# One V of each layer loads its last 512 columns in sixteen transfers of eight rows

## The chip, the cores and the metric

The kernel runs on one core of one Trainium2 chip. The metric is the time of one execution on the device in microseconds; of several executions the median is given. A profile of one execution gives what each engine did and when.

The engines named below are PE (TensorE, matmuls), DVE (VectorE), ACT (ScalarE), POOL (GpSimd) and SP (SyncE, which here only issues DMA transfers). Behind SP stand 16 transfer engines that move the bytes.

## The reference

One token goes through two layers, each an attention over a cache of 4096 positions in 32 heads and an MLP with a hidden width of 1376. All data are float32. Both layers read the same caches and weights.

```python
def _A_ref(x, k_cache, v_cache, wq, wo):
    q = (x @ wq).reshape(B, Sq, H, Dh).transpose(0, 2, 1, 3)
    scores = jnp.einsum("bhqd,bhkd->bhqk", q, k_cache) * (Dh ** -0.5)
    p = _softmax(scores, axis=-1)
    o = jnp.einsum("bhqk,bhkd->bhqd", p, v_cache)
    return o.transpose(0, 2, 1, 3).reshape(B, Sq, H * Dh) @ wo

def _B_ref(x, w1, b1, w2, b2):
    h = _gelu(jnp.einsum("bsd,df->bsf", x, w1) + b1)
    return jnp.einsum("bsf,fd->bsd", h, w2) + b2

x = x + _A_ref(_layernorm(x), ...)
x = x + _B_ref(_layernorm(x), ...)
...
```

(The last two lines are run twice.)

## The kernel before

The 32 heads are cut into G = 8 groups of four heads. A group's K is one block of 128 rows x 16384 columns (64 KiB a row, 8 MiB), laid out with the head's width on the rows; its V is a block of the same size with the cache's positions on the rows. Beside them come 2 MiB per group of query and output weights, called w. A block has C = 8 chunks of NC = 2048 columns, a chunk has four pieces of U = 512 columns, one per head or position block.

All of it lies in one SBUF tensor, `arena`, whose places are given by column: three homes of one block each, and behind them room for w and for scratch. `load` (L83) issues one transfer on SP into given columns of all 128 rows. Layer 0 goes through the groups upwards, layer 1 downwards, so that the last groups of layer 0 are reused; n counts the groups within a layer.

For each n the program does, in this order: load K of this group (issued ahead), `scores` (L213: 64 matmuls on PE, chunk by chunk), `softmax` (L217 to L233), load V and `values` (L241: again chunk by chunk), load w, `scaled_out` (L245 to L250), `head_out` (L269, reads wo), and `queries` for the next group (L203 to L208, reads wq). In layer 0 the homes of K and V go round among the three; in layer 1 V has home 0 and K home 1. `stream` (L356) issues a block's load and hands out its chunks; for a V in the middle of a layer it is a single transfer of the whole block (`WHOLE`).

SP takes its transfers in the order of the program, and each can carry waits: for readers of the place that it overwrites, and for a semaphore. The transfers of SP count on eight semaphores in turn, DMAHW0 to DMAHW7: transfer number i (from 0) counts on DMAHW(i mod 8), and before a semaphore is used again, the transfer that used it last must have landed. In the kernel before there are 79 transfers.

Of the kernel before, what the change touches and what calls it, by code (L numbers as in the profile page):

```python
# [23 lines left out]
C = 8  # L24
# [3 lines left out]
U = 512  # L28
KEPT = 6

NC = 4 * U
BLOCK = 8 * NC
# [21 lines left out]
WHOLE, HALVES = ((0, 8),), ((0, 4), (4, 8))  # L54
# [4 lines left out]
def decode_layers(ctx: ExitStack, tc: tile.TileContext, k, v, w, w1, w2, out):  # L59
    nc = tc.nc  # L60
# [20 lines left out]
    arena = const.tile([P, ARENA], F32, name="arena")  # L81

    def load(at, src):  # L83
        t = arena[:, at : at + src.shape[-1]]
        tc.keep_in_program_order(nc.sync.dma_start(t, src))
        return t
# [4 lines left out]
    def chunk(t, i=0):  # L91
        return t[:, NC * i : NC * (i + 1)].rearrange("p (j n) -> p j n", j=4)

    def of_w(first, n):

        row, i = first
        return w[row][:, AHEAD + NC * i : AHEAD + NC * (i + n)]

    def wq_at(g):
        return (g + 1) % 2, g  # L100

    def wo_at(g):
        return g % 2, g

    def free_now(layer, n):

        if layer == 0:
            at = HELD + 2 * NC
        elif n == 0:
            at = 6 * NC  # L110
            return arena[:, at : at + U], arena[:, 11 * NC : 11 * NC + 4 * 129]
        else:
            at = 9 * NC if n == 1 else 2 * BLOCK + NC
        return arena[:, at : at + U], arena[:, at + U : at + U + 4 * 129]
# [6 lines left out]
    def part(src, g, a, b):  # L121

        return src[g][:, NC * a : NC * b]
# [115 lines left out]
    def values(i, pt, vt, c, of=C):  # L239
        for j in range(J):  # L240
            nc.tensor.matmul(pO[32 * j : 32 * j + 4, :], pt[:, j, c, :], by_head(vt)[:, j],  # L241
                             start=(i == 0), stop=(i == of - 1))

    def scaled_out(rl, ot):
        nc.vector.transpose(ot[:, :512], pO)  # L245
        diag = ot.rearrange("p (b q) -> p b q", q=129)[:, :, :P]
        diag = diag.rearrange("p b (d q) -> p d b q", q=32)[:, :, :, 0]
        o, on = small("o", 4), small("on", 4)
        nc.vector.tensor_reduce(o, diag, axis=AX.X, op=ALU.add)
        nc.vector.tensor_scalar(on, o, rl, None, op0=ALU.mult)  # L250
        return on
# [101 lines left out]
    nc.gpsimd.tensor_copy(b2c, ahead[:, B2_AT : B2_AT + 4])  # L353
    here = {}

    def stream(what, g, pieces, base):  # L356

        for a, b in pieces:
            t = load(base + NC * a, part(k if what == "k" else v, g, a, b))
            for c in range(a, b):  # L360
                here[what, g, c] = chunk(t, c - a)
                yield c, here[what, g, c]

    w1_t = arena[:, HELD:PAIR]
    w2_t = [[arena[:, at : at + U] for at in homes] for homes in W2_AT]

    def idle(t, at, n=512):
        pin(nc.tensor.matmul(at[:C, :n], ident[:, :C], t[:, 0, :n], start=True, stop=True))  # L368

    for layer in range(2):  # L370
# [22 lines left out]
        for n, g in enumerate(order):  # L393
            first, final = n == 0, n == G - 1

            k_home, v_home = ((2 * n + i) % 3 * BLOCK for i in (1, 2))
            if layer == 1:
                k_home, v_home = K2_HOME if n == 2 else BLOCK, 0

            if layer == 1 and n == 0:  # L400
                tiles = [(c, here["k", g, c]) for c in range(C)]
            elif layer == 1 and n == 1:
                tiles = [(c, here["k", g, c]) for c in range(2)]
                tiles += list(stream("k", g, ((2, 4), (4, 8)), -2 * NC))
                n_kept = STAY + U * KEPT
                load(V1_HOME[6] + n_kept % NC, v[g][:, n_kept:BLOCK])
                for u in range(STAY, n_kept - U, U):
                    nc.scalar.copy(v_next(u), pK[(u - STAY) // U])
                for c in range(STAY // NC, C):
                    here["v", g, c] = chunk(arena[:, V1_HOME[c] : V1_HOME[c] + NC])  # L410
            elif layer == 1 and n == 2:
                tiles = [(c, here["k", g, c]) for c in range(6)]
                tiles += list(stream("k", g, ((6, 8),), 2 * BLOCK - 6 * NC))
            else:
                tiles = stream("k", g, HALVES if first or final else WHOLE, k_home)
# [5 lines left out]
            p, ot = free_now(layer, n)  # L421
# [7 lines left out]
            if layer == 1 and n == 0:  # L429
                for c in range(C):  # L430
                    values(c, pt, here["v", g, c], c)
            elif layer == 1 and n == 1:
                for c in range(C):
                    values(c, pt, here["v", g, c], c)

                for pieces, base in ((((0, 4),), K2_HOME), (((4, 6),), SPARE - 4 * NC)):
                    for _ in stream("k", order[2], pieces, base):
                        pass
            elif final:
                last_v = chunk(arena[:, v_home + BLOCK - NC : v_home + BLOCK])  # L440
                for _ in range(FILL - 1):
                    idle(t, pS)
                for c, t in stream("v", g, LAST, v_home):
                    values(c, pt, t, c, C - 1)
                    if c == C - 2:
                        others = scaled_out(rl, ot)
                    for _ in range(LAST_IDLE.get(c, 0)):
                        idle(t, pS)
                for a in (BLOCK - NC, BLOCK - NC // 2):
                    load(v_home + a, v[g][:, a : a + NC // 2])  # L450
                for c in range(C):
                    here["v", g, c] = chunk(arena[:, v_home + NC * c : v_home + NC * (c + 1)])
            else:
                for c, t in stream("v", g, WHOLE, v_home):
                    for i in range(KEPT - 1):
                        if layer == 0 and n == G - 2 and c == (STAY + U * i) // NC:
                            nc.scalar.copy(pK[i], t[:, STAY // U % J + i - J * (c - STAY // NC), :])
                    values(c, pt, t, c)
# [3 lines left out]
            elif final:  # L462
                at = PAIR + NC * layer
# [8 lines left out]
            else:  # L472
                t = load(PAIR, of_w(wo_at(g) if layer == 0 else wq_at(g - 1), 2))
# [23 lines left out]
        at = work.tile([P, P], F32, name="pt")  # L497
# [18 lines left out]
        if layer == 0:  # L516
# [4 lines left out]
            g = G - 2  # L521
# [53 lines left out]
```

## Time and profile before

| | |
|---|---|
| Time, median of 3 runs | 678.17 us (677.4 to 679.03) |
| Profiled execution, its own time | 677.63 us |
| Its span, first to last instruction | 675.9 us |
| Busy: PE, DVE, ACT, POOL | 408.1, 115.2, 27.4, 5.0 us |
| Read from HBM | 284.92 MB, 422 GB/s over the span |
| Chain that ended last, by engine | PE 40%, DMA 39%, unknown queue 14% |
| Granted TensorE clock, mean | 0.806 |

The views used are: the page's slices (the span in 40 equal parts, each digit the busy tenths), its rows on DMA queues and on DMA issues (KB each, median us from issue to landing), the windows (busy time of each engine in a stretch, then granted clock, DMA share and GB/s), the chain of waits in order of time (start, length, what), the timeline of SP (start, length of the issue, what it loads) and the list of who waited for whom. "Landing" is the moment at which the last of a transfer's engines has reported.

### The profile page before, as it was taken

What the parts mean: (1) busy time and instruction counts of PE and PEld (TensorE: products, weight loads), DVE (VectorE), ACT (ScalarE), POOL (GpSimd) and SP (SyncE); (2) the same over time, 40 slices, a digit from 0 to 9 for tenths busy, and PEclk for the clock granted to TensorE, in tenths of its full rate; (3) what the DMA queues carried; (4) which work ended last, traced back from release to release, by engine and by line L of the source; (5) the groups of instructions that cost most, each with busy time, mean ns of one, the idle gap of its engine ahead of it and who ended that gap; (6) DMA issues with size and microseconds to landing.
All of it is one profiled execution on the core that took longest, in us unless ns stands there. A gap on an engine that the chain in (4) does not pass through costs nothing.

```text
span 675.9 us, 6740 instructions
## 1 busy us (share of the span) xinstructions
PE 408.1 (60%) x3008; PEld 109.8 (16%) x3008; DVE 115.2 (17%) x369; ACT 27.4 (4%) x57; POOL 5.0 (1%) x24
## 2 busy tenths in 40 slices
PE   2745664565534854467597986674466545755596
PEld 1111111111111111111124321111111111111123
DVE  3002110120021201212022322120121111200212
ACT  0010000000000000001011200000000000000010
POOL 1000000000000000000000000000000000000000
PEclk9779776797678865878899998976797767976899
DMA  9999999999999999999999999999999999999995
GB/s 374 435 434 434 435 435 434 413 457 432 428 427 422 444 434 432 434 432 417 433 410 353 427 418 462 407 447 435 426 432 431 432 434 409 461 432 411 426 414 234
DMA packets 11268, 285.34 MB, mean 422 GB/s; under 512 B 1252, under 2 KB 1256, under 8 KB 3688
## 3 DMA queue, kind: packets, MB, share of 16 engines
q1 hardware_dynamic: 11240, 284.92, 98.6%
q8 instruction: 23, 0.38, 0.2%
q14 instruction: 5, 0.04, 0.0%
HBM read 284.92 MB, written 0.00 MB: 422 GB/s over the span
## 4 chain that ended last, share of the span: by engine, by line
PE 40%; DMA 39%; another core or an unknown queue 14%; DVE 4%; ACT 1%; issue 1%; ACTq 0%; SPq 0%; DVEq 0%
DMA arena<-in_v 35%; PE pO L241 19%; PE pS L213 12%; DMA arena<-in_w 4%; PE pB L269 4%; PE pO L207 1%; PE pO L225 1%; ACT arena L223 1%; PE pS L368 1%; DVE arena L245 1%; DVE smalls L217 1%; PE pO L368 0%; PE pO L343 0%; DVE arena L205 0%
## 5 line engine op out<-in xcount | busy, mean ns | idle before, releaser
L213 PE MATMUL pS<-arena,smalls 128*8 128x512 f32 x1024 | 148.3, 732 | 112.5 <-DMA arena<-in_k 111.6
L241 PE MATMUL pO<-arena,pt 128*4 128x512 f32 x1008 | 139.9, 700 | 79.1 <-DMA arena<-in_v 78.6
L269 PE MATMUL pB<-arena,smalls 128*1 128x512 f32 x112 | 52.8, 616 | 21.9 <-DVE smalls L250 15.9
L213 PEld LDWEIGHTS pS<-arena,smalls 128*8 128x8 f32 x1024 | 30.1, 103 | 214.9 <-issue 190.9
L241 PEld LDWEIGHTS pO<-arena,pt 128*4 128x4 f32 x1008 | 28.4, 95 | 178.0 <-issue 175.2
L217 DVE TENSOR_REDUCE smalls<-pS 128x1 f32<-128x512 f32 x16 | 11.1, 692 | 253.1 <-PE pS L213 253.1
L245 DVE STREAM_TRANSPOSE arena<-pO 128x512 f32<-128x512 f32 x16 | 11.5, 717 | 217.1 <-PE pO L241 217.1
L223 ACT ACTIVATE arena<-pS,smalls 128x512 f32<-128x512 f32 x16 | 12.4, 778 | 536.2 <-DVE smalls L222 536.2
L205 DVE SCALAR_TENSOR_TENSOR arena<-arena,smalls 128x512 f32<-128x512 f32 x45 | 33.8, 752 | 1.6
L225 PE MATMUL pO<-ident,arena 128*128 128x128 f32 x64 | 13.2, 341 | 33.8 <-ACT arena L223 33.5
L269 PEld LDWEIGHTS pB<-arena,smalls 128*1 128x1 f32 x112 | 8.6, 85 | 65.9 <-issue 38.2
L207 PE MATMUL pO<-smalls,arena 128*128 128x1 f32 x120 | 16.6, 259 | 3.3 <-DVE arena L205 3.3
L207 PEld LDWEIGHTS pO<-smalls,arena 128*128 128x128 f32 x120 | 15.3, 200 | 15.5 <-DVE arena L205 13.8
L225 PEld LDWEIGHTS pO<-ident,arena 128*128 128x128 f32 x64 | 8.5, 169 | 47.7 <-ACT arena L223 46.5
L368 PE MATMUL pO<-arena,ident 128*8 128x512 f32 (+1 forms) x38 | 15.9, 547 | 0.0
L368 PE MATMUL pS<-arena,ident 128*8 128x512 f32 (+1 forms) x34 | 14.0, 517 | 0.5 <-DVE pt L307 0.5
L203 DVE TENSOR_SCALAR arena<-arena,smalls 128x512 f32<-128x512 f32 x15 | 7.2, 480 | 4.7 <-DMA arena<-in_w 4.7
L343 PE MATMUL pO<-arena,smalls 128*1 128x128 f32 x176 | 5.9, 272 | 3.3 <-DMA arena<-in_w 2.2
L208 DVE COPY smalls<-pO 128x4 f32<-128x4 f32 x15 | 2.5, 165 | 26.5 <-PE pO L207 26.5
L169 PE MATMUL pO<-smalls 128*32 128x1 f32 x64 | 2.0, 184 | 7.4 <-DVE smalls L163 6.3
L229 DVE STREAM_TRANSPOSE smalls<-smalls 128x32 f32<-128x32 f32 x16 | 3.4, 211 | 17.5 <-ACT arena L223 17.5
L295 PE MATMUL pS<-arena,smalls 128*2 128x128 f32 (+1 forms) x160 | 4.9, 259 | 1.9 <-DMA arena<-in_w 1.9
(92 smaller groups left out, 101.2 us busy)
## 6 DMA issues: line engine op xcount, KB each, us to landing
arena<-in_k SPq DMA_DIRECT2D x8, 4096.0 KB, 26.0
arena<-in_w SPq DMA_DIRECT2D x13, 2048.0 KB, 33.2
arena<-in_v SPq DMA_DIRECT2D x2, 4096.0 KB, 38.4
arena<-in_k SPq DMA_DIRECT2D x3, 2048.0 KB, 15.9
arena<-in_v SPq DMA_DIRECT2D x2, 2048.0 KB, 41.6
arena<-in_w SPq DMA_DIRECT2D x4, 1024.0 KB, 16.3
arena<-in_w SPq DMA_DIRECT2D x6, 512.0 KB, 13.3
arena<-in_v SPq DMA_DIRECT2D x2, 1024.0 KB, 43.2
```

The source lines that it names most:

```text
L203: pin(nc.vector.tensor_scalar(t, wt[:, 0, :], xc[:, 0:1], None, op0=ALU.mult))
L205: nc.vector.scalar_tensor_tensor(t, wt[:, c, :], xc[:, c : c + 1], t, op0=ALU.mult, op1=ALU.add)
L207: nc.tensor.matmul(at[:, j : j + 1], t[:, P * j : P * (j + 1)], one, start=True, stop=True)
L213: nc.tensor.matmul(pS[32 * j : 32 * j + C, :], z[:, j, C - 1 - c : 2 * C - 1 - c], kt[:, j, :], start=(c == 0), stop=(c == C - 1))
L217: nc.vector.tensor_reduce(mx[:, 0:1], pS, axis=AX.X, op=ALU.max)
L223: nc.scalar.activation(p, pS, AF.Exp, bias=bias[:, 0:1], scale=sc, accum_out=mx[:, 0:1])
L225: nc.tensor.transpose(pT[:, b].rearrange("p j r -> p (j r)"), p[:, P * b : P * (b + 1)], ident)
L241: nc.tensor.matmul(pO[32 * j : 32 * j + 4, :], pt[:, j, c, :], by_head(vt)[:, j], start=(i == 0), stop=(i == of - 1))
L245: nc.vector.transpose(ot[:, :512], pO)
L269: nc.tensor.matmul(pB[0:1, :], on[:, d : d + 1], wt[:, d, :], start=n == 0 and d == 0, stop=n == G - 2 and d == 3)
L343: pin(nc.tensor.matmul(pM[32 * j : 32 * j + 1, :], g[:, c - b0 : c - b0 + 1], w2_t[c][:, P * j : P * (j + 1)], start=(c == 0), stop=(c == ...
L368: pin(nc.tensor.matmul(at[:C, :n], ident[:, :C], t[:, 0, :n], start=True, stop=True))
```

## The change

Two V blocks, that of n = 3 in layer 0 and that of n = 4 in layer 1, are loaded in another way. The first 15872 columns of all 128 rows come in one transfer. The last 512 columns (2 KiB a row) come in sixteen transfers of eight rows each. The rows of one transfer lie four partitions apart; sixteen starting rows, (p mod 4) + 32 x (p/4 mod 2) + 64 x (p/8), cover all 128 rows, the first eight transfers those below 64. The chunks are handed to `values` as before.

```diff
+    def spread(at, src):
+
+        for p in range(16):
+            first = p % 4 + 32 * (p // 4 % 2) + 64 * (p // 8)
+            rows = slice(first, first + 29, 4)
+            tc.keep_in_program_order(nc.sync.dma_start(arena[rows, at : at + src.shape[-1]], src[rows, :]))
+
...
+    def of_v(g, base, split):
+
+        if not split:
+            yield from stream("v", g, WHOLE, base)
+            return
+        load(base, v[g][:, : BLOCK - U])
+        spread(base + BLOCK - U, v[g][:, BLOCK - U : BLOCK])
+        for c in range(C):
+            yield c, chunk(arena[:, base + NC * c : base + NC * (c + 1)])
...
-                for c, t in stream("v", g, WHOLE, v_home):
+                for c, t in of_v(g, v_home, layer == 0 and n == 3 or layer == 1 and n == 4):
```

On SP, around n = 3 of layer 0, the order before reads as follows. Each row is a transfer with its place, source, rows x columns, and the semaphores that it waits for (DMAHW0 to 7 count landings; DVE, PE and the others count that engine's instructions). The rows are V of n = 3, w of n = 3, K and V of n = 4, and w of n = 4:

```order
L85 DMA arena<-in_v 128x16384 [waits DMAHW0_49,PE_49]
L85 DMA arena<-in_w 128x4096 [waits DMAHW2_49,DVE_49,PE_49]
L85 DMA arena<-in_k 128x16384 [waits DMAHW1_49]
L85 DMA arena<-in_v 128x16384 [waits DMAHW3_49,PE_49]
L85 DMA arena<-in_w 128x4096 [waits DMAHW5_49,DVE_49,PE_49]
```

Nothing stands there between V and w. In the change, the same place on SP begins so. The large V is transfer number 12 and counts on DMAHW4; the small ones are numbers 13 to 28 and count on DMAHW5, 6, 7, 0, 1 and so on:

```order
L85 DMA arena<-in_v 128x15872 [waits DMAHW0_49,PE_49]
L361 DMA arena<-in_v 8x512 [waits DVE_49,PE_49]
L361 DMA arena<-in_v 8x512 x3
L361 DMA arena<-in_v 8x512 [waits DMAHW1_49]
L361 DMA arena<-in_v 8x512 [waits DMAHW2_49]
L361 DMA arena<-in_v 8x512 [waits DMAHW3_49]
L361 DMA arena<-in_v 8x512 [waits DMAHW4_49]
L361 DMA arena<-in_v 8x512 [waits DMAHW5_49]
L361 DMA arena<-in_v 8x512 [waits DMAHW6_49]
```

The eighth small one is the one that waits for DMAHW4, on which the large V counts. Further on, still on SP, the train ends with its 14th to 16th transfer, and w of n = 3, K and V of n = 4 and w of n = 4 follow:

```order
L361 DMA arena<-in_v 8x512 [waits DMAHW2_49]
L361 DMA arena<-in_v 8x512 [waits DMAHW3_49]
L361 DMA arena<-in_v 8x512 [waits DMAHW4_49]
L85 DMA arena<-in_w 128x4096 [waits DMAHW5_49,DVE_49,PE_49]
L85 DMA arena<-in_k 128x16384 [waits DMAHW6_49]
L85 DMA arena<-in_v 128x16384 [waits DMAHW7_49,PE_49]
L85 DMA arena<-in_w 128x4096 [waits DMAHW0_49,DMAHW5_49,DVE_49,PE_49]
```

Here w and K, which directly followed V before, stand behind all sixteen small transfers, and wait for the landings of the 9th and the 10th. In layer 1 the order is alike, with the large V on DMAHW1 and the eighth small one waiting for DMAHW1.

On PE, `values` of n = 3 in the change is cut once more. The rows are the first matmul of the group, its next 27, the first of the eighth chunk, and the last three; then `head_out` follows:

```order
L241 MATMUL pO<-arena,pt 4x512 [waits DMAHW4_49,DVE_49]
L241 MATMUL pO<-arena,pt 4x512 x27
L241 MATMUL pO<-arena,pt 4x512 [waits DMAHW4_49,DMAHW5_49,DMAHW3_49,DMAHW6_49,DMAHW2_49,DMAHW7_49,DMAHW1_49,DMAHW0_49]
L241 MATMUL pO<-arena,pt 4x512 x3
L269 MATMUL pB<-arena,smalls 1x512 [waits DMAHW5_49,DVE_49]
```

Before, the first row was followed by 31 matmuls without a wait; now the 29th waits for all eight semaphores. (Each matmul of the order is two in the profile's count.)

## The prediction

> **What bounds the kernel now.** I read the slices of the page first, then the windows, then the chain of waits in order of time, then SP's timeline.
>
> ```profile
> DMA  9999999999999999999999999999999999999995
> GB/s 374 435 434 434 435 435 434 413 457 432 428 427 422 444 434 432 434 432 417 433 410 353 427 418 462 407 447 435 426 432 431 432 434 409 461 432 411 426 414 234
> ...
> DMA packets 11268, 285.34 MB, mean 422 GB/s; under 512 B 1252, under 2 KB 1256, under 8 KB 3688
> ...
> q1 hardware_dynamic: 11240, 284.92, 98.6%
> ```
>
> The transfer engines are busy in every slice, at about 434 GB/s. One queue, q1, that of SP, carries all of the kernel's data. The windows say the same of layer 1 from 380 to 640 us (the last two numbers are the DMA share and GB/s), while PE is busy for 156 of the 260 us:
>
> ```profile
> 380.00:640.00 260.00, 156.16 (x1018) 39.30 (x1016) 43.60 (x130) 8.72 (x19) 0.00 (x0) 0.80 1.00 432
> ```
>
> So time is bytes over 434 GB/s, and each microsecond in which the queue stands empty is lost, unless another engine is late anyway. The chain around the first changed V (layer 0, n = 3) shows that none is; the gaps called "unknown queue" are PE waiting for a landing:
>
> ```profile
> 201.14 9.03 PE pS L213 x64
> ...
> 213.53 6.83 another core or an unknown queue
> 220.37 0.14 issue
> 220.50 9.59 PE pO L241 x64
> ...
> 235.94 8.69 another core or an unknown queue
> 244.63 0.14 issue
> 244.76 5.48 PE pS L213 x25
> ```
>
> V lands at 220.4; PE multiplies it, then waits 8.7 us for K of n = 4. A later K makes PE later by the same amount. Around the second place (layer 1, n = 4) it is alike:
>
> ```profile
> 496.21 33.75 DMA arena<-in_v
> 529.96 0.14 issue
> 530.10 8.39 PE pO L241 x64
> ```
>
> What keeps the queue full is that SP issues far ahead:
>
> ```profile
> 166.13 0.33 SPq L85 DMA_DIRECT2D arena<-in_v  x1
> 191.97 0.33 SPq L85 DMA_DIRECT2D arena<-in_w  x1
> 192.35 0.42 SPq L85 DMA_DIRECT2D arena<-in_k  x1
> ...
> 496.21 0.33 SPq L85 DMA_DIRECT2D arena<-in_v  x1
> 502.07 0.33 SPq L85 DMA_DIRECT2D arena<-in_w  x1
> 520.29 0.33 SPq L85 DMA_DIRECT2D arena<-in_k  x1
> ```
>
> When V lands at 220.4, w and K of 10 MiB have stood behind it for 28 us. When V lands at 530.0, w has waited for 28 us and K for 10 us.
>
> **The change, step by step.** Bytes stay the same. Per layer one V of 8 MiB loses 256 KiB, which come in sixteen issues.
>
> *The added waits.* The order of SP shows them: from the 5th (layer 0) or the 6th (layer 1) on, each small transfer waits for one of the eight DMA semaphores. The semaphores go round in turn, and a transfer waits until the one eight places earlier has landed. The transfer eight places before the 8th small one is the large V itself (DMAHW4 in layer 0, DMAHW1 in layer 1). So SP stands at the 8th until the large V has landed. Behind it stand eight more small ones, w, K and the next V, everything that has filled the queue so far. At that landing only small ones 1 to 7 (112 KiB, a fraction of a microsecond) are still queued; then the transfer engines have nothing. The waits of the 5th to 7th end earlier (the 7th's in layer 0 with K of n = 3, before PE's scores start at 201.14) and cost nothing by themselves, since nothing but the rest of the train and w stands behind them, and w came only at 191.97 before, held by this:
>
> ```profile
> SPq L85 <- DVE arena L205: 23.6, 1, 23.6
> ```
>
> *The issues after the landing.* Nine small issues (8 to 16) go out before w. The trace has no 8-row issue. Its nearest rows:
>
> ```profile
> 0.72 0.39 SPq L85 DMA_DIRECT2D arena<-in_w  x1
> 1.18 0.88 SPq L85 DMA_DIRECT2D arena<-in_k  x2
> ...
> 673.29 0.65 SPq L528 DMA_DIRECT2D out<-arena  x1
> ```
>
> Issues of 128 rows follow each other every 0.45 us at the start (0.72 to 1.18) and every 0.38 at 191.97 to 192.35. The only issue with fewer than 16 rows, the 4-row store of the output, takes 0.65 instead of 0.33 us. In it the packets under 512 B count: 78 x 16 + 4 = 1252, one completion packet for each engine of 78 transfers, and four for the store. An 8-row transfer is of that kind, so I take 0.65 + 0.05 between issues = 0.70 us: 9 x 0.70 = **6.3 us**. Ends: 9 x 0.38 = 3.4, and 9 x 0.80 = 7.2 if a back-to-back issue adds to 0.65 the 0.1 by which 192.35's 0.42 exceeds 191.97's 0.33, plus the gap.
>
> *The restart.* w then meets an empty queue. The page's first transfer did so too; beside it the 768 KB one of 364.13, met by a nearly empty queue (the second row is used further down):
>
> ```profile
> arena<-in_w SPq DMA_DIRECT2D x1, 1056.0 KB, 4.9
> ...
> q8 instruction: 1, 0.02, 1.3%
> ...
> arena<-in_w SPq DMA_DIRECT2D x1, 768.0 KB, 5.1
> ```
>
> 1056 KB at 434 GB/s are 2.5 us, so 4.9 - 2.5 = **2.4 us** of start and landing that a full queue hides; the other row gives 5.1 - 1.8 = 3.3, the upper end. The lower end is 1.9, if half a microsecond of the first one was a cold start (an estimate).
>
> *What is saved.* The large V is 256 KiB shorter: 0.6 us at 434 GB/s, and the small ones travel in the gap.
>
> Per place: 6.3 + 2.4 - 0.6 = **8.1 us** (ends 4.7 and 9.9); two places give 16.2 (9.4 to 19.8).
>
> *What lies beside it.* PE needs small one 16 only for the eighth chunk (its last four L241 matmuls wait for all eight semaphores): issued 5.6 us after the landing, landed by 8.0, while seven eighths of 9.59 and 8.39 us are 8.4 and 7.3. At most 0.7 us of wait, and that is covered, because L269 behind it waits for w until 6.3 + 2.4 + 4.8 = 13.5 us after the landing. From there L269 and L207 take some 4.6 us, but K lands 19.3 us after w, so PE waits for K as before. SP's next w is due after L207, with K still under way. The queue is full again and nothing else starves. After 220 and after 530 the transfers run at full rate to the end of the layer, so neither loss is regained.
>
> *The engines' spread.* The end of the run shows that the 16 engines don't finish together:
>
> ```profile
> 668.00:672.00 4.00, 2.42 (x79) 1.70 (x72) 0.73 (x3) 0.41 (x2) 0.08 (x1) 1.00 0.21 84
> ...
> DMA  1100000000000000000000000000000000000000
> GB/s 68 68 0 27 27 27 27 27 27 27 27 0 0 0 0 0 0 0 0 0 0 0 0 0 0 0 0 0 0 0 14 0 0 0 0 0 0 0 0 0
> ```
>
> From 668 on only a fifth of the engines work, and from 670 (second view, 670 to 676 us) a single one at 27 GB/s. The last one decides each landing. [...] One such 16 KB fetch holds its engine for 1.3% of 16 x 5 us = 1.0 us (the q8 row above, of 364 to 369 us). I add 1.0 us once, for the end of the run; bounds 0 and 2.0.
>
> Sum: 677.6 (the profiled execution) + 16.2 + 1.0 = 694.8; the median of the runs shown is 678.2, half a microsecond above that execution, so I say **695.0**. Ends: 677.6 + 9.4 = 687.0 and 677.6 + 19.8 + 2.0 = 699.4.
>
> **Rivals.**
>
> *Small issues are cheap.* Eight rows cost SP no more than 128: 9 x 0.45 = 4.05, so 5.85 per place, 677.6 + 11.7 + 1.0 = **690.3**. For it: most issue rows. Against it: the only short transfer's 0.65. Chance 0.30, beside 0.58 for my forecast.
>
> *The balance pays (other side).* [...] Chance 0.07, of which 0.03 beyond 0.2% (1.4 us, about what a measurement of this kernel can tell from no change), since 1.2 us lies just within.
>
> [...]
>
> *Each small one costs a round trip.* If each of the nine were issued only when the one before had landed, each would cost the 2.4 us of an empty queue: 9 x 2.4 + 2.4 - 0.6 = 23.4 per place, **724**. Against it: the order lets the 9th wait for the 1st, not the 8th; and at 0.72, 1.18 and 1.6 us three transfers go out before the first lands at 5.6. Chance 0.05.
>
> [...]
>
> **Chances.** The forecast and the cheap-issue case hold 0.88 and span 687 to 699.4, so the range is 687.5 to 699.5. Slower by over 0.2%: 0.58 + 0.30 + 0.05 = 0.93; within: 0.04; faster: 0.03.
>
> **What would show it.** SP's timeline: the 8th small issue some 0.05 us after the large V has landed, then nine issues 0.70 us apart (0.45 by the cheap rival), w and K directly behind them. Windows just after the two landings: a DMA share near zero for 5 us or more. The packets under 512 B: 1252 + 32 x 8 = 1508 with eight engines each (1764 with sixteen). Elsewhere the chain's pieces keep their lengths. I am wrong if w's issue stands ahead of the large V's landing, or if the queue never empties.

## The result, and the profile after

The changed kernel takes 693.94 us (median of 4 runs, 693.17 to 694.28) against 678.01 us before (677.4 to 679.03): a ratio of 1.0232, 95% interval 1.0214 to 1.025. The forecast was 695.0, in a range of 687.5 to 699.5. The profiled execution took 693.17 us, 15.54 more than the one profiled before.

The page of the changed kernel, its slices and its rows on DMA:

```profile
DMA  9999999999599999999999999999998699999997
GB/s 394 454 425 425 430 425 429 451 438 412 213 425 428 460 444 424 423 422 428 426 410 377 419 423 439 423 459 436 425 423 382 253 425 425 426 440 431 424 414 282
DMA packets 11780, 285.34 MB, mean 413 GB/s; under 512 B 1508, under 2 KB 1512, under 8 KB 4200
...
q1 hardware_dynamic: 11752, 284.93, 96.5%
```

The bytes are the same; q1's share is down from 98.6 to 96.5%, and there are two notches in the rate, at the 11th slice (213 GB/s) and the 31st and 32nd (382 and 253). They are the two places. The packets under 512 B are 1508 = 1252 + 32 x 8: eight for each small transfer, read here as one from each of eight engines.

SP's timeline around both places (start, length of the issue or of the group of issues, what it loads):

```profile
176.00 5.97 SPq L361 DMA_DIRECT2D arena<-in_v  x9
182.08 0.37 SPq L85 DMA_DIRECT2D arena<-in_w  x1
182.50 0.42 SPq L85 DMA_DIRECT2D arena<-in_k  x1
...
503.30 0.33 SPq L85 DMA_DIRECT2D arena<-in_v  x1
504.27 38.75 SPq L361 DMA_DIRECT2D arena<-in_v  x16
543.12 0.37 SPq L85 DMA_DIRECT2D arena<-in_w  x1
```

Nine small issues from 176.00 to 181.97, one every 0.67 us, and w directly behind them. At the second place the sixteen end at 504.27 + 38.75 = 543.02; seen by themselves, the last nine begin at 537.05 there, again one every 0.67 us. PE shows what released them: its first matmuls on V come at 176.12 and 537.17, so the large V had just landed. The rows are of the changed kernel, V and then K of the next group, at each place:

```profile
176.12 2.74 PE L241 MATMUL pO<-arena,pt 128*4 128x512 f32 x12 [6.84 <-DMA arena<-in_v]
...
208.87 3.64 PE L213 MATMUL pS<-arena,smalls 128*8 128x512 f32 x20 [12.32 <-DMA arena<-in_k]
...
537.17 9.75 PE L241 MATMUL pO<-arena,pt 128*4 128x512 f32 x64 [6.13 <-DMA arena<-in_v]
...
570.66 1.90 PE L213 MATMUL pS<-arena,smalls 128*8 128x512 f32 x8 [12.68 <-DMA arena<-in_k]
```

The same rows of the kernel before (the row of 530.10 stands in the forecast; K of the first place is its 201.14):

```profile
176.88 1.89 PE L241 MATMUL pO<-arena,pt 128*4 128x512 f32 x8 [7.40 <-DMA arena<-in_v]
...
554.36 1.90 PE L213 MATMUL pS<-arena,smalls 128*8 128x512 f32 x8 [10.02 <-DMA arena<-in_k]
```

At the first place V comes 0.76 us sooner and K of the next group 7.73 us later (208.87 - 201.14). At the second, V comes 7.07 us later and K 16.30. So the first place costs 7.73 us and the second 16.30 - 7.73 = 8.57: between the landing of V and that of the next K they lose 8.49 (7.73 + 0.76) and 9.23 (16.30 - 7.07), of which the sooner landing of the shorter V gives back 0.76 and 0.66. The windows in which next to nothing flows, and one of the end (changed kernel; the last two numbers are the DMA share and GB/s):

```profile
176.00:183.00 7.00, 6.88 (x44) 1.41 (x48) 0.00 (x0) 0.00 (x0) 0.00 (x0) 0.65 0.08 23
537.00:544.00 7.00, 6.83 (x40) 1.35 (x44) 0.00 (x0) 0.00 (x0) 0.00 (x0) 0.60 0.08 23
684.00:688.00 4.00, 3.32 (x128) 2.62 (x123) 1.43 (x6) 0.62 (x3) 0.76 (x4) 1.00 0.50 200
```

For 7 us the transfer engines are at 8%, while PE works on V. The third row is the end of the run, used below.

### The profile page after: what moved, and what is told of

It is laid out like the page before. It is cut to its first block, busy times and chain, and to the rows that moved or that the text cites. A ratio compares the mean times of both kernels' runs of the same rounds, so it can differ in the third digit from the quotient of the medians.

```text
span 691.4 us, 6795 instructions
## 1 busy us (share of the span) xinstructions
PE 406.9 (59%) x3008; PEld 109.2 (16%) x3008; DVE 115.0 (17%) x369; ACT 27.4 (4%) x57; POOL 5.0 (1%) x24
## 2 busy tenths in 40 slices
DMA packets 11780, 285.34 MB, mean 413 GB/s; under 512 B 1508, under 2 KB 1512, under 8 KB 4200
## 3 DMA queue, kind: packets, MB, share of 16 engines
q1 hardware_dynamic: 11752, 284.93, 96.5%
## 4 chain that ended last, share of the span: by engine, by line
DMA 53%; PE 28%; another core or an unknown queue 13%; DVE 3%; SPq 2%; issue 1%; ACT 1%; ACTq 0%; DVEq 0%
DMA arena<-in_v 49%; PE pO L241 15%; PE pS L213 7%; DMA arena<-in_w 5%; PE pB L269 3%; SPq L361 1%; PE pO L207 1%; PE pO L225 1%; PE pO L343 1%; DVE arena L245 1%; ACT arena L223 1%; PE pS L385 0%; DVE smalls L217 0%; PE pO L385 0%
## 5 line engine op out<-in xcount | busy, mean ns | idle before, releaser
L213 PE MATMUL pS<-arena,smalls 128*8 128x512 f32 x1024 | 142.8, 708 | 121.5 <-DMA arena<-in_k 120.6
L241 PE MATMUL pO<-arena,pt 128*4 128x512 f32 x1008 | 138.5, 700 | 84.6 <-DMA arena<-in_v 84.2
L269 PE MATMUL pB<-arena,smalls 128*1 128x512 f32 x112 | 57.3, 660 | 25.4 <-DVE smalls L250 13.2
L225 PE MATMUL pO<-ident,arena 128*128 128x128 f32 x64 | 11.8, 314 | 34.1 <-ACT arena L223 33.8
L269 PEld LDWEIGHTS pB<-arena,smalls 128*1 128x1 f32 x112 | 9.0, 89 | 73.2 <-issue 49.9
L385 PE MATMUL pO<-arena,ident 128*8 128x512 f32 (+1 forms) x38 | 15.9, 547 | 0.0
```

Of the source, the lines that this page charges most:

```text
L213: nc.tensor.matmul(pS[32 * j : 32 * j + C, :], z[:, j, C - 1 - c : 2 * C - 1 - c], kt[:, j, :], start=(c == 0), stop=(c == C - 1))
L225: nc.tensor.transpose(pT[:, b].rearrange("p j r -> p (j r)"), p[:, P * b : P * (b + 1)], ident)
L269: nc.tensor.matmul(pB[0:1, :], on[:, d : d + 1], wt[:, d, :], start=n == 0 and d == 0, stop=n == G - 2 and d == 3)
```

## The experiments

Theory A is that of the forecast: the 8th small transfer waits for the large V on their common semaphore, SP stands, the queue empties; what is lost are the issues between that landing and w, and a restart. Rival B: the small transfers cost time on the transfer engines by themselves. Rival C: SP's issues and waits cost by themselves, whatever is queued. All edits are made on the changed kernel, in `spread`, in the two calls in `of_v` or where `of_v` is called; "..." marks lines that are left out. Each ratio is to runs of the kernel before, made beside the run.

### Fewer, larger pieces, and more, smaller ones

`four_by_32`, `eight_by_16`: rows p, p + n, p + 2n, ... of n transfers. The edit is that of `four_by_32`; `eight_by_16` has `n = 8` and `n * 15` in place of `n * 31`.

```diff
-        for p in range(16):
-            first = p % 4 + 32 * (p // 4 % 2) + 64 * (p // 8)
-            rows = slice(first, first + 29, 4)
+        n = 4
+        for p in range(n):
+            rows = slice(p, p + n * 31 + 1, n)
```

> The last 512 columns of the two V come in four transfers of 32 rows instead of sixteen of eight; everything else is as in the change. Theory A (the 8th small transfer waits for the large V, so the queue empties): with four there is no 8th, no wait on the large V, and SP issues w and K ahead as before, so 677.5 to 679. Rival B (each small transfer has a price of its own on the transfer engines, 15.9 us / 32 = 0.5 us): eight of them cost 4 us, 682.

Measured: 678.13 us against 677.91, ratio 1.0006 (0.9995 to 1.0016). No loss, as theory A has it; rival B's 682 is out.

> Eight transfers of 16 rows. Theory A: only the 8th waits for the large V; behind the landing come one issue of 0.45 us and the restart of 2.4 us, less 0.6 saved, 2.3 us for each place, 682.5 (681 to 684). Rival B: 16 x 0.5 = 8 us, 686. If the restart cost nothing and only the issues did: 679.

Measured: 684.32 us, ratio 1.0098 (1.0083 to 1.0113), a little over theory A's bound (684) and below rival B (686); by itself it hardly parts the two. SP's timeline and PE's, of an execution that took 685.61 us, the longest of the four:

```profile
143.03 34.11 SPq L361 DMA_DIRECT2D arena<-in_v  x8
177.25 0.52 SPq L85 DMA_DIRECT2D arena<-in_w  x1
...
205.58 4.94 PE L213 MATMUL pS<-arena,smalls 128*8 128x512 f32 x32 [13.79 <-DMA arena<-in_k]
```

Eight issues of 16 rows, the last just before w at 177.25; one issue instead of nine stands behind the landing, and the loss by K is 4.44 us (205.58 - 201.14) instead of 7.73. From w's issue to K it takes 28.3 us, where 10 MiB at 434 GB/s take 24.2: a restart of 4.0 (with the 0.14 from a landing to PE's start taken off), more than the 2.4 expected. At the second place it is 3.3 (563.01 - 535.38 - 24.2 - 0.14). One fetch of instructions (queue q8) falls into each of the two stretches, and none of that queue into those of the change, whose restarts are 2.5 and 3.2. But the second places hardly differ all the same (3.3 and 3.2), so the cause stays open.

`thirtytwo`: 32 transfers of eight rows x 256 columns.

```diff
-        for p in range(16):
-            first = p % 4 + 32 * (p // 4 % 2) + 64 * (p // 8)
-            rows = slice(first, first + 29, 4)
+        for p in range(32):
+            first = p // 2 % 4 + 32 * (p // 8 % 2) + 64 * (p // 16)
+            rows, a = slice(first, first + 29, 4), U // 2 * (p % 2)
...
-            tc.keep_in_program_order(nc.sync.dma_start(arena[rows, at : at + src.shape[-1]], src[rows, :]))
+            tc.keep_in_program_order(nc.sync.dma_start(arena[rows, at + a : at + a + U // 2], src[rows, a : a + U // 2]))
```

> Thirty-two transfers of eight rows x 256 columns. Theory A: 25 issues instead of 9 come between the landing and w, 16 x 0.67 us more for each place: 693.9 + 21.4 = 715.3. Rival B with half the bytes each: between 693.9 (price by bytes) and 710 (price by transfer). If each waited for a round trip of 2.4 us: 770.

Measured: 715.34 us (2 runs, 715.16 to 715.53), ratio 1.0552 (1.0531 to 1.0573). Theory A's number; the bytes are the same, the issues behind the landing are 25. SP comes to w at 192.92 instead of 182.08 (16 issues, 0.68 us each), and in the window up to there the transfer engines are at 5%:

```profile
192.92 0.37 SPq L85 DMA_DIRECT2D arena<-in_w  x1
...
176.00:193.00 17.00, 9.05 (x56) 1.61 (x56) 0.00 (x0) 0.00 (x0) 0.00 (x0) 0.70 0.05 13
```

`layer0_only`: the change at n = 3 of layer 0 alone.

```diff
-                for c, t in of_v(g, v_home, layer == 0 and n == 3 or layer == 1 and n == 4):
+                for c, t in of_v(g, v_home, layer == 0 and n == 3):
```

> The change at its first place alone (layer 0, n = 3). Theory A: one of two equal losses, 678 + 8 = 686. If the loss of layer 0 were regained before the end and only that of layer 1 counted: 678.

Measured: 685.41 us (2 runs) against 678.02, ratio 1.0106 (1.0087 to 1.0124): 7.4 us, about half the loss of 15.9. Layer 0's loss is not regained, and the rest, 8.5, is what the second place adds.

### The wait with a full queue behind it

`sixteen_wide`: sixteen transfers again, of all rows x 512 columns.

```diff
         for p in range(16):
-            first = p % 4 + 32 * (p // 4 % 2) + 64 * (p // 8)
-            rows = slice(first, first + 29, 4)
-            tc.keep_in_program_order(nc.sync.dma_start(arena[rows, at : at + src.shape[-1]], src[rows, :]))
+            load(at + U * p, src[:, U * p : U * (p + 1)])
...
-        load(base, v[g][:, : BLOCK - U])
-        spread(base + BLOCK - U, v[g][:, BLOCK - U : BLOCK])
+        load(base, v[g][:, : BLOCK - 16 * U])
+        spread(base + BLOCK - 16 * U, v[g][:, BLOCK - 16 * U : BLOCK])
```

> Sixteen transfers again, but each of all 128 rows x 512 columns (256 KiB), so that the first V transfer has half the block. The 8th still waits for that half, and nine issues still stand ahead of w. Theory A: at that landing seven transfers (1.75 MiB, 4.2 us) are queued, more than one issue and a restart, and each further issue of 0.45 us brings 0.6 us of data, so the queue does not empty: 677.5 to 680. Rival C (the issues and waits of SP cost by themselves, whatever is queued): 2 x (9 x 0.45 + 2.4) = 13 us, 691. Rival B: 32 x 0.5, 694.

Measured: 680.88 us, ratio 1.0044 (1.0029 to 1.0059). Rivals B and C (694, 691) are out: nine issues and the wait are there and cost almost nothing, since some 4 us of data (seven transfers of 256 KiB at 434 GB/s, an estimate) are queued at the landing. The 3 us that stay, about one above theory A's bound, go with a lower rate while the rows of 2 KiB flow:

```profile
168.00:176.00 8.00, 6.58 (x60) 1.71 (x60) 1.01 (x6) 0.87 (x2) 0.00 (x0) 1.00 1.09 403
```

In windows this short the share has to be read beside the GB/s. In the kernel before, two neighbouring windows of 2 us read 131 and 524 GB/s, but at shares of 0.30 and 1.21, so that GB/s over share is 437 and 433:

```profile
158.00:160.00 2.00, 2.00 (x16) 0.43 (x12) 0.00 (x0) 0.00 (x0) 0.00 (x0) 0.50 0.30 131
160.00:162.00 2.00, 2.00 (x20) 0.38 (x16) 0.00 (x0) 0.00 (x0) 0.00 (x0) 0.82 1.21 524
```

In the window of `sixteen_wide` it is 403 / 1.09 = 370, some 15% below 434. Over the 8 us that is 1.3 us (8 x 1.09 x 0.15, an estimate), and twice that is most of the 3 us.

`interleaved`: the sixteen small transfers unchanged, in three trains between three parts of V.

```diff
-    def spread(at, src):
-
-        for p in range(16):
+    def spread(at, src, which):
+
+        for p in which:
...
-        load(base, v[g][:, : BLOCK - U])
-        spread(base + BLOCK - U, v[g][:, BLOCK - U : BLOCK])
+        end = BLOCK - U
+        for (a, b), which in (((0, 2 * NC), range(5)), ((2 * NC, 5 * NC), range(5, 10)), ((5 * NC, end), range(10, 16))):
+            load(base + a, v[g][:, a:b])
+            spread(base + end, v[g][:, end:BLOCK], which)
```

> All sixteen transfers of eight rows at both places, in SP's queue, with the same rows and columns as in the change, but the rest of V comes in three transfers (2, 3 and 2.75 MiB) that stand between them: part, 5 small, part, 5 small, part, 6 small. Every wait for a part then ends while the next part (3 MiB, 7.3 us, or 2.75 MiB) or w is still queued. Theory A: the queue never empties, 677.5 to 679, although the small transfers, their issues and their waits are all there. Rival B (the small transfers cost by themselves) and rival C (SP's issues cost by themselves): 690 or more. [...]

Measured: 680.41 us, ratio 1.0035 (1.0021 to 1.0048). All sixteen small transfers, their issues and their eight-places-back waits are there, at both places, and 13.2 of the 15.9 us are gone. So what the change loses is, for the most part, the empty queue. What stays is 2.7 us, 1.4 above theory A's upper end, and no gain. The rate around the trains says where (by the bytes queued ahead of them, at 434 GB/s from K's landing at 157, they flow at about 162, 169 and 176, an estimate):

```profile
160.00:162.00 2.00, 2.00 (x16) 0.50 (x12) 0.00 (x0) 0.00 (x0) 0.00 (x0) 0.50 1.13 466
162.00:167.00 5.00, 4.98 (x48) 0.95 (x36) 0.00 (x0) 0.00 (x0) 0.00 (x0) 0.97 0.99 423
167.00:170.00 3.00, 0.26 (x1) 0.26 (x2) 1.76 (x7) 0.87 (x2) 0.00 (x0) 0.86 0.99 367
...
175.00:178.00 3.00, 3.00 (x28) 0.63 (x24) 0.00 (x0) 0.00 (x0) 0.00 (x0) 0.84 1.00 333
```

The engines are busy all the time, and yet GB/s over share falls to 333 at the third train and 371 at the second; at the first it is 412, close to 434. The first train holds rows of the lower 64 partitions, the second three transfers of the lower and two of the upper, the third rows of the upper 64. By these four windows the first place loses about 1.3 us (share x length x what the rate lacks of 434, an estimate). K of the next group comes 2.27 us later there (203.41 - 201.14), so a part of what stays is not accounted for.

`interleaved_2u`: 1024 columns in the small transfers (`end = BLOCK - 2 * U` in the edit above).

> [...]

Measured: 683.73 us, ratio 1.0085 (1.0071 to 1.0098). With twice the bytes in the small transfers the loss is 6.1 us instead of 2.7; neither run is faster than the kernel before.

`interleaved_rev`: the small transfers in the opposite order (the edit is against `interleaved`).

```diff
-        for p in which:
+        for p in (15 - q for q in which):
```

> As interleaved, with the sixteen small transfers in the opposite order: the eight of the upper 64 partitions first (five in the first train, three in the second), then the eight of the lower ones. [...] Rival E (a train is slow because of what stands next to it, the last part of V and w): the low rates stay at 175 to 178 us as in interleaved (333 GB/s).

Measured: 681.26 us, ratio 1.005 (1.0034 to 1.0067), and the same windows:

```profile
160.00:162.00 2.00, 2.00 (x16) 0.50 (x12) 0.00 (x0) 0.00 (x0) 0.00 (x0) 0.50 1.12 373
162.00:167.00 5.00, 5.00 (x44) 1.00 (x36) 0.00 (x0) 0.00 (x0) 0.00 (x0) 0.87 1.00 423
167.00:170.00 3.00, 0.42 (x4) 0.00 (x0) 1.51 (x5) 0.73 (x2) 0.00 (x0) 1.00 1.08 416
...
175.00:178.00 3.00, 2.60 (x28) 0.51 (x24) 0.00 (x0) 0.00 (x0) 0.00 (x0) 1.00 0.95 365
```

GB/s over share is 333 at the first train (412 in `interleaved`), 385 at the second (371) and 384 at the third (333). If rows of the upper 64 partitions are slow wherever they stand, the low rate goes with them to the first train, and it did. But the third train, now of lower rows alone, recovered only to 384, where the lower rows had 412 in the first train of `interleaved`, and the second, now with three transfers of upper rows in place of two, did not get slower. So part of it belongs to the place, and rival E is not wholly out.

### What an issue costs, and two other ways to move the bytes

`sixteen_of_16`: same number and bytes, 16 rows each.

```diff
-            first = p % 4 + 32 * (p // 4 % 2) + 64 * (p // 8)
-            rows = slice(first, first + 29, 4)
-            tc.keep_in_program_order(nc.sync.dma_start(arena[rows, at : at + src.shape[-1]], src[rows, :]))
+            rows, a = slice(p // 2, p // 2 + 121, 8), U // 2 * (p % 2)
+            tc.keep_in_program_order(nc.sync.dma_start(arena[rows, at + a : at + a + U // 2], src[rows, a : a + U // 2]))
```

> Sixteen transfers of 16 rows x 256 columns: same number, same bytes, same waits as the change, but each uses all sixteen engines. Theory A with the price of a short transfer's issue (0.67 us with 8 rows, 0.45 with 16 or more): 9 x 0.22 = 2.0 us less for each place, 693.9 - 4.0 = 690. If the issue takes 0.67 for any transfer that small: 693.9.

Measured: 695.3 us, ratio 1.0252 (1.0238 to 1.0266). The reason that the forecast gave for the price of an issue, that fewer than 16 rows take longer, is wrong. (A transfer of 16 rows leaves sixteen packets under 512 B: `eight_by_16` has 1508 = 1252 + 16 x 16.) Nine issues of 16 rows take as long as nine of eight, 6.05 us against 5.97. The first row is this run's, the second that of `four_by_32`, the third that of `balance_3`, below, whose three transfers (112, 8 and 8 rows) have adjacent rows, and the fourth that of one transfer of `sixteen_wide` (128 adjacent rows of 2 KiB):

```profile
176.69 6.05 SPq L360 DMA_DIRECT2D arena<-in_v  x9
```

```profile
143.46 2.46 SPq L361 DMA_DIRECT2D arena<-in_v  x4
```

```profile
123.43 1.07 SPq L359 DMA_DIRECT2D arena<-in_v  x3
```

```profile
121.59 0.43 SPq L85 DMA_DIRECT2D arena<-in_v  x1
```

That is 0.67, 0.61, 0.36 and 0.43 us an issue. What the long ones share, with the output's store of four rows 32 apart (0.65), is the step between rows; the 8-row transfers with adjacent rows are short, and so are those with rows of 2 KiB. No pair of runs changes the step alone.

`balance_3`: the last 4096 columns in three transfers, one of 112 rows and two of eight.

```diff
-        for p in range(16):
-            first = p % 4 + 32 * (p // 4 % 2) + 64 * (p // 8)
-            rows = slice(first, first + 29, 4)
+        for rows in (slice(0, 112), slice(112, 120), slice(120, 128)):
             tc.keep_in_program_order(nc.sync.dma_start(arena[rows, at : at + src.shape[-1]], src[rows, :]))
...
-        load(base, v[g][:, : BLOCK - U])
-        spread(base + BLOCK - U, v[g][:, BLOCK - U : BLOCK])
+        load(base, v[g][:, : BLOCK - 8 * U])
+        spread(base + BLOCK - 8 * U, v[g][:, BLOCK - 8 * U : BLOCK])
```

> [...] Three transfers bring no wait on the large V. Theory A: 677 to 679. [...]

Measured: 692.77 us, ratio 1.0218 (1.0202 to 1.0233), far from theory A's 677 to 679. SP has issued w and K long before (147.51 and 147.92), and the queue is full; but the rate falls while these three transfers flow:

```profile
160.00:170.00 10.00, 7.36 (x56) 1.51 (x48) 1.51 (x5) 0.80 (x2) 0.00 (x0) 0.84 1.03 428
170.00:174.00 4.00, 2.04 (x12) 0.98 (x16) 1.13 (x6) 0.07 (x1) 0.00 (x0) 0.51 0.93 225
174.00:178.00 4.00, 4.00 (x32) 0.74 (x28) 0.00 (x0) 0.00 (x0) 0.00 (x0) 0.64 1.11 229
178.00:182.00 4.00, 2.27 (x24) 0.34 (x16) 0.00 (x0) 0.00 (x0) 0.00 (x0) 1.00 0.86 131
182.00:186.00 4.00, 2.19 (x12) 0.45 (x16) 0.00 (x0) 0.00 (x0) 0.00 (x0) 0.71 1.06 438
```

So slow transfers are a second way to lose nearly as much as the change does (14.8 us), with the queue full. The 524 KB of the 4 us from 178 on are twice what the two transfers of eight rows hold (2 x 128 KiB), so other rows flowed beside them; the windows don't part the three transfers.

`on_pool`: the sixteen transfers issued by POOL.

```diff
-            tc.keep_in_program_order(nc.sync.dma_start(...))
+            tc.keep_in_program_order(nc.gpsimd.dma_start(...))
```

> The same sixteen transfers of eight rows at both places, issued by POOL instead of SP. They count on semaphores of POOL's own, so SP's order is that of the kernel before: w and K are issued ahead and nothing on SP waits for a small transfer. Theory A: the loss is gone, 677 to 679.5. Rival B (the small transfers themselves cost): 694. [...]

Measured: 728.62 us, ratio 1.0754 (1.0736 to 1.0771). It tells nothing on theory A, because POOL's own train became the last: beside SP's full queue its issues come mostly one in 9 to 10 us, though the first eight carry no wait on one another. Once SP's queue has run empty (31 GB/s from 216 to 235), they come one in 2.2 us, as in the third row.

```profile
154.64 0.53 POOL L361 DMA_DIRECT2D arena<-in_v  x1 [8.87 <-issue]
164.70 0.52 POOL L361 DMA_DIRECT2D arena<-in_v  x1 [9.54 <-issue]
...
224.88 0.52 POOL L361 DMA_DIRECT2D arena<-in_v  x1 [1.65 <-issue]
```

What holds them was not tried.

No version is faster than the kernel before; `four_by_32` alone is level with it.

## Why the prediction was right, step by step

**What bounds the kernel, and no cover:** right. The losses of the two places in the profile, 16.3 us, come back in the end time, 15.9 by the medians; `layer0_only` shows 7.4 for one place.

**A row misread.** For the first place the forecast took the rows of n = 4 (V issued at 166.13, landed at 220.4) for those of n = 3, whose V is issued at 123.83 and lands before 176.88. The two groups have the same pattern, so no term changed, but the times at which the notch was expected were one group off, and PE's row of 201.14 is K of the next group, not of n = 3.

**The added wait:** right, and shown: the 8th issue comes at the landing at both places; with four pieces there is no loss, with the queue filled behind the wait 2.7 to 3.0 us of 15.9 (`interleaved`, `sixteen_wide`).

**Nine issues, 6.3 us:** measured 6.1 (176.00 to 182.08, 0.67 each against 0.70). The size was right, the reason wrong, and so the size was luck: by every run here the step between the rows, not their number, goes with a long issue, and the store from which the price was taken happens to have one.

**The restart, 2.4 us:** from w's issue to PE's first matmul on K it takes 26.8 us at the first place and 27.5 at the second (208.87 - 182.08, 570.66 - 543.12). 10 MiB at 434 GB/s are 24.2, PE starts 0.14 after a landing: 2.5 and 3.2, inside the bounds of 1.9 and 3.3. The 4.0 of `eight_by_16` lies outside, so the bounds were too narrow.

**Saved, 0.6 us:** V's first matmul came 0.76 us sooner at the first place, and 0.66 at the second, beside what it is late by (7.73 - 7.07).

**Per place 8.1 us:** 7.73 and 16.30 - 7.73 = 8.57, together 16.3 where 16.2 was forecast.

**PE's wait for w:** right. L269, which reads w, was put at 13.5 us after V's landing; it starts 13.5 us after the 8th issue (189.50 - 176.00), and PE still waits 12.3 us for K behind it (the row of 208.87).

```profile
189.50 6.06 PE L269 MATMUL pB<-arena,smalls 128*1 128x512 f32 x8 [4.01 <-DMA arena<-in_w]
```

**The engines' spread, +1.0 us:** not seen, and no run shows that an emptied queue brings the 1.0 us of a fetch to the end of the run; the term was an estimate of the forecast. What the runs showed in its place is a shorter end. The profiled executions differ by 15.54 us, 0.8 less than the two places lost. The difference lies in the last w, which takes 12.0 instead of 13.3 us from issue to landing; before, one engine alone works from 670 on and the last 4 us have a share of 0.21, after, the last 4 us have 0.50 (chain of waits, the changed kernel first):

```profile
675.79 12.02 DMA arena<-in_w
```

```profile
658.91 13.33 DMA arena<-in_w
```

An emptied queue is not needed for the shorter w: in `four_by_32`, where none emptied, the same row reads 12.0, and in `interleaved`, where none emptied either, 13.5.

```profile
660.16 12.01 DMA arena<-in_w
```

```profile
661.86 13.53 DMA arena<-in_w
```

All thirteen profiled executions have 11.9 to 12.0 or 13.3 to 13.5 there; those with an emptied queue have 12.0, the others both. So the +1.0 was not seen in any of them, and whether a restart plays a part in the shorter w is open. The forecast of 695.0 lies 1.1 us above the measured 693.94, about this term. (The stated range adds 0.5 and 0.1 us to the ends of its sum, 687.0 and 699.4; nothing hangs on that.)

**The rivals.** "Small issues are cheap" fell by 0.67 us an issue. "The balance pays", the faster side, has no run for it: no version became faster, and where the queue stays full (`interleaved`, `interleaved_2u`) the loss rises from 2.7 to 6.1 us with the bytes in the small transfers. Whether the small transfers leave any engine with more or fewer bytes was not shown, since the traces carry no engine numbers. "Each a round trip" fell by the nine issues 0.67 us apart. The packet count, 1508, is the one forecast for eight engines a transfer.

## What to carry to other kernels

In a kernel that lives on a full queue, count the transfers between two large ones: where completion semaphores go round in turn, eight of them here, the eighth transfer after a large one waits for it (here it was issued at 176.00, 0.12 us before PE's first matmul on the large V), and everything behind stands with it. Look at the order for a wait on the large transfer's own semaphore, and keep the train shorter than that, or keep enough bytes queued behind it (here an issue every 0.6 to 0.7 us and 2.5 to 4 us of restart had to be covered). Whatever another cut of a block into transfers is to bring has to be weighed against one emptied queue, some 8 us here, and against the rate at which the reshaped transfers run (14.8 us lost in `balance_3`).

## What the hardware showed that was not expected

How the rows were divided among transfers changed the rate, even with the engines busy. With one transfer of 112 adjacent rows of 16 KiB and two of eight in flight, the rate was 225 to 229 GB/s for 8 us and 131 for 4, beside 428 before and 438 after (`balance_3`). While trains of eight rows four apart flowed, GB/s over share was 333 where the rows were all of the upper 64 partitions, and 384 to 412 where they were all of the lower ones (`interleaved`, `interleaved_rev`).

In the mixed second trains it was 371 with two transfers of upper rows and 385 with three, so there more upper rows did not slow them. What makes the rate differ, no run shows.

An issue on SP of rows with a step between them took 0.61 us (`four_by_32`, 32 rows) to 0.70 (`interleaved`, 8 rows) as the mean of a train, of adjacent rows 0.33 to 0.52 (8 to 128 rows).
